# The four convolution products of the second token group: from VectorE to GpSimd

## Chip, cores and metric

The kernel runs on one core of a Trainium2 chip. The metric is the device time of one execution in microseconds (us), lower is better; three runs of the kernel before are given with their median.

## The reference

What is computed is a convolution with weights of its own for each token, followed by a two-layer MLP. Cut to what matters:

```python
# x [4, 4096, 192], weight_gen [4, 4096, 8, 7]
w = softmax(weight_gen, axis=-1)              # 7 taps for each token and head
x_unf = x_pad[:, idx, :]                      # the token and the 6 before it
out = einsum('bshk,bskhg->bshg', w, x_unf)    # g = 24 channels a head
h = out.reshape(16384, 192) @ w_in            # w_in [192, 2048]
g = s * max(h, 0) ** 2 + b
return g @ w_out                              # w_out [2048, 192]
```

Everything is float32. The kernel holds each factor of a matmul as a rounded part and a rest, and adds three products.

## The kernel before

The 16384 tokens are cut into 32 groups of 512. For each group the convolution is formed on 128 partitions (4 quarters of the channels times 32 runs of 16 tokens), turned, split into its two parts, and then multiplied with `w_in` (the tiles `ph`), passed through relu and square on ScalarE (`r`, `gh`) and VectorE (`gl`), and multiplied with `w_out` (the tiles `po`). The 2048 hidden channels are taken in four quads of 512, each of two pairs of 128.

The order on every engine is the order of the program text, written out by hand. There are three stretches that matter here:

- The first group (index 0) has a convolution of its own kind, with TensorE (`first_pieces`).
- While the first group goes through the MLP, in the loop `for i in range(NC)` with its eight turns, the weights are converted as they arrive: `convert(i)` splits the tile of weights `r` into `wc`'s two parts, with five instructions on VectorE (lines 239, 243, 247, 254 and 258; from the sixth tile on a sixth, line 266), three on ScalarE (236, 252, 277) and a few matmuls (276). Turn `i` of the loop also holds the pair's matmuls (`mm1_pair`, lines 542 and 548, and `mm2_pair`, line 634), relu and square (578, 582, 586) and `low_g` (604). A pair's second matmul group trails the first by one turn.
- Between these, the convolution of the second group (index 1) is laid by the tuple `beside`, which says which of the group's pieces follow each turn.

From the second group's MLP on, the loop `for n in range(NQ, last + 1)` runs 124 quads of the same kind (`mm1_quad`, line 567, and `mm2_quad`, line 652), each with some pieces of the convolution of a later group.

The convolution's pieces are in `conv_pieces(g)`. `products(h, k0, k1)` multiplies the shifted input `xt` by the tap weights `w` into the tile `pr`, for one of the two heads of each quarter and the taps k0 to k1: 4 taps by 16 tokens by 24 channels, 1536 elements a partition, or 3 taps, 1152. There are four such instructions a group (line 351). `add` sums the taps. For the second group alone, where `by_dma` is true, the adds are DMAs from GpSimd's queue that accumulate into `pr` (line 363), and the pieces stand in this order:

```python
softmax_a, exp, softmax_b,
products(0, 0, 4), products(1, 0, 4), add(0, 2, 2), products(0, 4, 7), products(1, 4, 7),
add(4, 5), add(0, 1), add(4, 6), last_add,
transposes, split_hi, split_lo,
```

with

```python
beside = ((0, 3), (3, 4), (4, 6), (6, 11), (11, 11), (11, 13), (14, 15), (15, 15))
```

so the softmax follows turn 0, the first product turn 1, the second product and the first DMA turn 2, the last two products and the other three DMAs turn 3, and the last add (line 376) with the transposes (387, 392) turn 5.

Of the kernel before, what the change touches and what calls it, by code (L numbers as in the profile page):

```python
# [20 lines left out]
def dynamic_conv_then_relu2_mlp(  # L21
# [24 lines left out]
    nc = tc.nc  # L46
# [264 lines left out]
    def conv_pieces(g):  # L311
        st = {}
        by_dma = g == 1
# [29 lines left out]
        def products(h, k0, k1):  # L343
            def f():
                if "pr" not in st:
                    st["pr"] = conv.tile([P, K, J, FQ], F32, tag="pr", name="pr")
                xt, w, pr = xt_t[g], st["w"], st["pr"]
                xs = xt[:, k0:k0 + 1, h * G:h * G + 1]
                ws = w[:, 0:1, h:h + 1, k0:k0 + 1]
                n = k1 - k0  # L350
                nc.vector.tensor_tensor(  # L351
                    out=pr[:, k0:k1, :, h * G:(h + 1) * G],
                    in0=bass.AP(xs.tensor, xs.offset, [xs.ap[0], [FQ, n], [FQ, J], [1, G]]),
                    in1=bass.AP(ws.tensor, ws.offset, [ws.ap[0], [1, n], [HQ * K, J], [0, G]]),
                    op=ALU.mult,
                )
            return f
# [464 lines left out]
```

## Time and profile before

| | us |
|---|---|
| median of three runs | 1161.42 |
| lowest, highest run | 1161.0, 1163.08 |
| span of the profiled execution, first to last instruction | 1161.6 |

The profiled execution's own time is not listed apart from the three runs; its span is 0.2 us over their median.

How to read it: the profile lists instructions by engine. PE is TensorE's matmuls and PEld its weight loads, DVE is VectorE, ACT is ScalarE, POOL is GpSimd, SP is SyncE, which issues most DMAs. L351 is line 351 of the kernel. Times are counted from the span's start. "Idle before" a row is how long its engine had stood still, and the arrow names what it waited for. POOL's spans are rough.

### The profile page before, as it was taken

What the parts mean: (1) busy time and instruction counts of PE and PEld (TensorE: products, weight loads), DVE (VectorE), ACT (ScalarE), POOL (GpSimd) and SP (SyncE); (2) the same over time, 40 slices, a digit from 0 to 9 for tenths busy, and PEclk for the clock granted to TensorE, in tenths of its full rate; (3) what the DMA queues carried; (4) which work ended last, traced back from release to release, by engine and by line L of the source; (5) the groups of instructions that cost most, each with busy time, mean ns of one, the idle gap of its engine ahead of it and who ended that gap; (6) DMA issues with size and microseconds to landing.
All of it is one profiled execution on the core that took longest, in us unless ns stands there. A gap on an engine that the chain in (4) does not pass through costs nothing.

```text
span 1161.6 us, 29979 instructions
## 1 busy us (share of the span) xinstructions
PE 1142.1 (98%) x12724; PEld 1125.3 (97%) x12724; DVE 943.1 (81%) x1346; ACT 848.9 (73%) x898; POOL 9.7 (1%) x28
## 2 busy tenths in 40 slices
PE   7999999999999999999999999999999999999997
PEld 5679999999999999999999999999999999999997
DVE  6988888878898878898878898887888887888854
ACT  3867777777777777777777777777777777777774
POOL 0000000000000000000000000000000000000000
PEclk9999999999999999999999999999999999999999
DMA  5651122212122212112212112222212221212110
GB/s 150 160 92 40 29 41 47 46 33 47 25 37 46 47 34 47 26 37 47 47 33 46 29 36 45 47 43 37 38 31 41 47 47 33 47 25 38 24 25 15
DMA packets 171738, 52.33 MB, mean 45 GB/s; under 512 B 160148, under 2 KB 163860, under 8 KB 171604
## 3 DMA queue, kind: packets, MB, share of 16 engines
q1 hardware_dynamic: 171028, 48.45, 21.2%
q0 software_dynamic: 576, 1.97, 0.9%
q8 instruction: 100, 1.64, 0.6%
q14 instruction: 34, 0.28, 0.1%
HBM read 27.70 MB, written 12.58 MB: 35 GB/s over the span
## 4 chain that ended last, share of the span: by engine, by line
PE 94%; DVE 3%; DMA 1%; ACT 1%; issue 0%; SPq 0%; DVEq 0%
PE po L652 48%; PE ph L567 43%; PE po L634 1%; PE po L457 1%; DVE gl L604 1%; DVE pr L351 1%; DMA r<-in_moe_w_in_dram 0%; DVE r L247 0%; DMA x<-in_x_dram 0%; DVE v L258 0%; DVE t L254 0%; PE ph L542 0%; PE ph L276 0%; PE po L476 0%; DVE t L243 0%
## 5 line engine op out<-in xcount | busy, mean ns | idle before, releaser
L652 PE MATMUL po<-wc,gh 64*128 64x384 f32 x3936 | 596.2, 354 | 0.3 <-DVE y L669 0.3
L652 PEld LDWEIGHTS po<-wc,gh 64*128 64x128 f32 x3936 | 570.9, 184 | 0.8 <-DVE y L669 0.6
L652 PE MATMUL po<-wc,gl 64*128 64x192 f32 x3936 | 550.0, 249 | 0.0
L652 PEld LDWEIGHTS po<-wc,gl 64*128 64x128 f32 x3936 | 549.1, 187 | 0.1
L604 DVE SCALAR_TENSOR_TENSOR gl<-r,shift,gh 128x1024 fp32r<-128x1024 f32 x256 | 327.0, 1278 | 185.3 <-ACT gh L586 183.5
L578 ACT ACTIVATE r<-ph 128x1024 f32<-128x1024 f32 x254 | 247.2, 1023 | 264.5 <-PE ph L567 260.9
L567 PE MATMUL ph<-xa,wc 64*128 64x512 f32 x2976 | 374.9, 387 | 0.0
L567 PEld LDWEIGHTS ph<-xa,wc 64*128 64x128 f32 x2976 | 343.0, 184 | 1.2 <-ACT r L582 0.3
L586 ACT ACTIVATE gh<-r,shift 128x1024 fp32r<-128x1024 f32 x254 | 292.8, 1153 | 8.1
L582 ACT ACTIVATE r<-r 128x1024 f32<-128x1024 f32 x254 | 267.2, 1052 | 0.2
L567 PE MATMUL ph<-xb,wc 64*128 64x512 f32 x1488 | 205.0, 386 | 0.1
L351 DVE TENSOR_TENSOR pr<-xt,w 128x1536 f32<-128x1536 f32 (+1 forms) x124 | 187.5, 1552 | 1.6 <-DVE w L336 0.4
L567 PEld LDWEIGHTS ph<-xb,wc 64*128 64x128 f32 x1488 | 179.1, 184 | 0.8 <-issue 0.5
L368 DVE TENSOR_TENSOR pr<-pr 128x1536 f32<-128x1536 f32 (+1 forms) x120 | 136.1, 1154 | 2.1
L664 DVE TENSOR_SCALAR u<-po,ratio 128x192 f32<-128x192 f32 x128 | 49.7, 409 | 2.0 <-PE po L634 1.9
L669 DVE SCALAR_TENSOR_TENSOR y<-po,ratio,u 128x192 f32<-128x192 f32 x128 | 49.6, 408 | 0.1
L376 DVE TENSOR_TENSOR acc<-pr 128x768 f32<-128x768 f32 x31 | 29.7, 958 | 1.0
L387 DVE STREAM_TRANSPOSE xT<-acc 128x128 f32<-128x128 f32 x124 | 27.6, 280 | 1.1
L392 DVE STREAM_TRANSPOSE xT<-acc 128x128 f32<-128x128 f32 x124 | 26.3, 270 | 0.0
L634 PE MATMUL po<-wc,gh 128*128 128x384 f32 x80 | 24.4, 369 | 0.0
L405 DVE TENSOR_TENSOR xb<-xT,xb 128x512 fp32r<-128x512 f32 x31 | 21.2, 685 | 0.0
L405 DVE TENSOR_TENSOR xa<-xT,xa 128x512 fp32r<-128x512 f32 x31 | 21.2, 685 | 0.0
(67 smaller groups left out, 346.0 us busy)
## 6 DMA issues: line engine op xcount, KB each, us to landing
xt<-in_x_dram SPq DMA_DIRECT2D x120, 132.0 KB, 3.1
out_dram<-y SPq DMA_DIRECT2D x124, 96.0 KB, 1.9
xb<-xb SPq DMA_DIRECT2D x124, 64.0 KB, 2.0
wg<-in_weight_gen_dram SPq DMA_DIRECT2D x124, 28.0 KB, 2.6
r<-in_moe_w_out_dram SPq DMA_DIRECT2D x8, 384.0 KB, 4.2
r<-in_moe_w_in_dram SPq DMA_DIRECT2D x12, 128.0 KB, 6.0
pr<-pr POOLq DMA_DIRECT2D x3, 384.0 KB, 4.3
r<-in_moe_w_in_dram SPq DMA_DIRECT2D x32, 32.0 KB, 2.8
```

Source lines behind the costliest of these rows:

```text
L351: nc.vector.tensor_tensor(out=pr[:, k0:k1, :, h * G:(h + 1) * G], in0=bass.AP(xs.tensor, xs.offset, [xs.ap[0], [FQ, n], [FQ, J], [1, G]]), ...
L368: nc.vector.tensor_tensor(out=pr[:, o:o + n], in0=pr[:, o:o + n], in1=pr[:, a:a + n], op=ALU.add)
L405: nc.vector.tensor_tensor(out=x[h][:, 1], in0=xT[:, h], in1=x[h][:, 0].bitcast(F32), op=ALU.subtract)
L567: nc.tensor.matmul(out=h_t[n, p][:, j], lhsT=w1(2 * k + p, part, block, j, rows), rhs=v[rows], start=(at < 2 and c == 0), stop=(at >= 4 an ...
L578: nc.scalar.activation(out=r[p], in_=h_t.pop((n, p)), func=AF.Relu)
L582: nc.scalar.activation(out=r[p], in_=r[p], func=AF.Square)
L586: nc.scalar.activation(out=gh, in_=r[p], func=AF.Identity, bias=shift)
L604: nc.vector.scalar_tensor_tensor(out=gl, in0=sq, scalar=shift, in1=gh.bitcast(F32), op0=ALU.add, op1=ALU.subtract)
L634: nc.tensor.matmul(**m)
L652: nc.tensor.matmul(**m)
L664: nc.vector.tensor_scalar(out=u[i], in0=o_t[g][tiles[i]][:, 1, :], scalar1=ratio, scalar2=None, op0=ALU.mult)
L669: nc.vector.scalar_tensor_tensor(out=y[:, t], in0=o_t[g][t][:, 0, :], scalar=ratio, in1=u[i - 1], op0=ALU.mult, op1=ALU.add,)
```

## The change

In `products`, the multiplication is issued on GpSimd for the second group, and on VectorE for the groups from the third on, as before. Operands, pieces and `beside` stay as they are.

```diff
@@ -348,7 +348,7 @@
                 xs = xt[:, k0:k0 + 1, h * G:h * G + 1]
                 ws = w[:, 0:1, h:h + 1, k0:k0 + 1]
                 n = k1 - k0
-                nc.vector.tensor_tensor(
+                (nc.gpsimd if by_dma else nc.vector).tensor_tensor(
                     out=pr[:, k0:k1, :, h * G:(h + 1) * G],
                     in0=bass.AP(xs.tensor, xs.offset, [xs.ap[0], [FQ, n], [FQ, J], [1, G]]),
                     in1=bass.AP(ws.tensor, ws.offset, [ws.ap[0], [1, n], [HQ * K, J], [0, G]]),
```

On VectorE, after turns 1 and 2 of the loop over the weight tiles, one product stood each time between `low_g` (L604) and the next tile's conversion (L239 and on); shown is the place after turn 2, the one after turn 1 reads alike.

```order
 L258 SCALAR_TENSOR_TENSOR v<-r,t 128x768
 L604 SCALAR_TENSOR_TENSOR gl<-r,shift,gh 128x1024
-L351 TENSOR_TENSOR pr<-xt,w 128x64x24
 L239 TENSOR_SCALAR t<-t 128x768
 L243 TENSOR_SCALAR t<-t 128x768
```

The product is gone there, and the conversion follows `low_g` directly. After turn 3 VectorE had the last two products in the same place:

```order
 L266 TENSOR_TENSOR rest<-r,wc_110 128x768
 L604 SCALAR_TENSOR_TENSOR gl<-r,shift,gh 128x1024
-L351 TENSOR_TENSOR pr<-xt,w 128x48x24 x2
 L239 TENSOR_SCALAR t<-t 128x768
 L243 TENSOR_SCALAR t<-t 128x768
```

On GpSimd, whose own order has nothing else between the identity matrix of the start (`eye_f`) and the DMAs that add, the four products come in ahead of the DMAs that read them.

```order
 L282 ISA
 L282 AFFINE_SELECT eye_f<-ones_f 128x128
+L351 TENSOR_TENSOR pr<-xt,w 128x64x24 x2
 L363 DMA pr<-pr 128x1536
+L351 TENSOR_TENSOR pr<-xt,w 128x48x24 x2
 L363 DMA pr<-pr 128x768 x3
 L162 MEMSET xt 1x288 x16
```

GpSimd is not held back by the turns of the loop as VectorE's order was: its first product is due as soon as the tap weights `w`, the input `xt` and the tile `pr` are ready.

## Rows read from the trace of the kernel before

**Rows 1.** Page, part 1: busy us, share of the span and instructions, by engine.

```profile
PE 1142.1 (98%) x12724; PEld 1125.3 (97%) x12724; DVE 943.1 (81%) x1346; ACT 848.9 (73%) x898; POOL 9.7 (1%) x28
```

**Rows 2.** Windows: stretch, length, busy by engine (instructions), TensorE clock, DMA share, GB/s.

```profile
40.00:50.00 10.00, 10.00 (x52) 7.29 (x51) 9.69 (x11) 8.20 (x11) 0.00 (x0) 1.00 0.53 155
50.00:60.00 10.00, 9.09 (x54) 7.58 (x54) 9.76 (x12) 8.33 (x9) 1.40 (x2) 1.00 0.74 127
60.00:70.00 10.00, 7.48 (x37) 6.16 (x35) 9.62 (x13) 6.29 (x7) 2.22 (x3) 0.83 0.78 151
```

**Rows 3.** Chain that ended last, 42 to 92 us: start, length, engine, line.

```profile
42.72 1.67 DVE pr L351
...
49.30 1.67 DVE pr L351
...
56.75 2.54 DVE pr L351 x2
...
64.02 1.62 PE ph L276 x4
...
91.90 4.07 PE po L652 x26
```

**Rows 4.** Timeline of PE, 41 to 79 us: start, length, count, [idle before, releaser].

```profile
41.09 0.94 PE L276 MATMUL ph<-r,eye_f 128*128 128x384 f32 x2
...
55.70 0.41 PE L276 MATMUL ph<-rest,eye 128*128 128x384 f32 x1 [0.91 <-DVE rest L266]
...
64.02 0.66 PE L276 MATMUL ph<-rest,eye 128*128 128x384 f32 x1 [2.52 <-DVE rest L266]
...
68.43 1.56 PE L542 MATMUL ph<-xa,wc 128*128 128x512 f32 x6
...
70.81 0.44 PE L276 MATMUL ph<-rest,eye 128*128 128x384 f32 x1
...
73.86 1.55 PE L542 MATMUL ph<-xa,wc 128*128 128x512 f32 x6
...
78.67 3.04 PE L567 MATMUL ph<-xa,wc 64*128 64x512 f32 x24
```

**Rows 5.** Windows of 1 us, columns as in rows 2: the clock around the longest stall.

```profile
62.00:63.00 1.00, 0.00 (x0) 0.00 (x0) 0.95 (x2) 0.28 (x1) 0.00 (x0) 1.00 1.16 224
63.00:64.00 1.00, 0.00 (x0) 0.01 (x1) 1.00 (x3) 0.96 (x2) 0.00 (x0) 0.79 1.03 197
64.00:65.00 1.00, 0.98 (x3) 1.00 (x4) 1.00 (x2) 0.97 (x2) 0.84 (x1) 0.50 1.05 203
66.00:67.00 1.00, 1.00 (x6) 1.00 (x5) 0.96 (x2) 1.00 (x2) 0.00 (x0) 0.50 1.04 203
67.00:68.00 1.00, 1.00 (x9) 1.00 (x8) 0.86 (x3) 1.00 (x2) 0.00 (x0) 1.00 0.50 92
```

**Rows 6.** Timeline of DVE, columns as in rows 4: from the tap weights on.

```profile
37.38 0.40 DVE L336 TENSOR_TENSOR w<-e,sm 128x224 f32<-128x224 f32 x1
37.69 0.55 DVE L239 TENSOR_SCALAR t<-t 128x768 f32<-128x768 f32 x1
...
40.57 0.96 DVE L258 SCALAR_TENSOR_TENSOR v<-r,t 128x768 fp32r<-128x768 uint32 x1
41.45 1.28 DVE L604 SCALAR_TENSOR_TENSOR gl<-r,shift,gh 128x1024 fp32r<-128x1024 f32 x1
...
70.77 0.95 DVE L376 TENSOR_TENSOR acc<-pr 128x768 f32<-128x768 f32 x1
```

**Rows 7.** Timeline of POOL, columns as in rows 4: all that it computes before 241 us.

```profile
0.85 0.10 POOL L178 MEMSET space<- 128x1 f32 x1
0.88 0.21 POOL L281 MEMSET ones_f<- 128x128 f32 x1
1.16 0.29 POOL L282 TENSOR_SCALAR_AFFINE_SELECT eye_f<-ones_f 128x128 f32<-128x128 f32 x1
...
51.60 1.00 POOL L363 DMA_DIRECT2D pr<-pr  x1 [50.15 <-DVE t L239]
59.60 1.76 POOL L363 DMA_DIRECT2D pr<-pr  x2 [7.00 <-DVE pr L351]
64.16 0.86 POOL L363 DMA_DIRECT2D pr<-pr  x1 [2.79 <-DMA pr<-pr]
```

**Rows 8.** Line 363, the adding DMAs: time from issue to landing.

```profile
DMA to landing us min/median/max: 3.8/4.8/6.7
```

## The prediction

> **What bounds the kernel now.** I read the page's busy times first, then the same by windows, then the chain that ended last, then single rows. The page shows PE busy for 98% of the span and POOL for 1% [rows 1], so from there a change of VectorE's load would seem to be worth nothing. The windows show that this is an average: between 40 and 70 us VectorE is busy 9.69, 9.76 and 9.62 us of each 10, while PE falls from 10.00 to 7.48 [rows 2]. In the chain all four products of the second group lie on the path: 1.67, 1.67 and 2.54 us, 5.88 in all, the last of them before the matmul that PE begins at 64.02 [rows 3]. From 91.90 us on the chain is the quads' matmuls, to the end. So whatever the change does is decided between 37 and 79 us, and what PE gains or loses at the first quad (78.67 us, rows 4) is handed to the end: the waits between 79 and 92 us hang on PE's own results, and nothing that the change touches lies there.
>
> **What the change removes.** VectorE loses 5.88 us of chain. PE can take less than that, because it takes only its own losses. These are its two stalls on VectorE, 0.91 us at 55.70 and 2.52 us at 64.02 [rows 4], and the slow clock that follows the second: granted 0.79 in the last microsecond of the stall and 0.50, the 1.2 GHz level, for the three that follow, 1.00 again from 67 [rows 5]. What that clock costs is read from the same work at both levels: from the conversion matmul to the next pair's first is 64.02 to 68.43, 4.41 us, and a turn later 70.81 to 73.86, 3.05 us [rows 4]. The difference is 1.36. The sum is 0.91 + 2.52 + 1.36 = **4.79 us**, the most that I give the change. Late next would be PE itself. The loss of cover elsewhere costs nothing: with the products gone, the adding DMAs start earlier, not later, and the last add that reads them stands at 70.77 [rows 6].
>
> **What it adds.** Four products on GpSimd, two of 1536 elements a partition and two of 1152. No row shows a product there, so I bound it by the nearest rows [rows 7]. Below: memset writes 1 element in 0.10 us and 128 in 0.21, 0.87 ns an element, which makes 1.43 and 1.10 us, 5.1 us for four. The only GpSimd row that also reads a tensor is the select, 0.29 us for 128 elements; in proportion 3.48 and 2.61 us, **12.2 us** for four. Above: the product reads two tensors, and on VectorE 768 elements take 0.96 us with two (L258) against 0.55 with one (L239) [rows 6], 1.75 times as long; that ratio on 12.2 makes 21.3 us. I take 12.2, the row that does most of the same work. The Trainium skill, "GPSIMD Engine Reference", section 3.1, speaks against moving elementwise work there: it gives 4497 ns for an addition of 2048 elements, from which I estimate 3.4 and 2.5 us, 11.8 us for four; by it the forecast below would be 0.4 us lower. No run here shows that figure yet.
>
> **Whether GpSimd's time is its own.** For dependencies it is. The tap weights are ready at 37.78 us (37.38 + 0.40, rows 6) and GpSimd has nothing else to do. The first two products would end at 37.78 + 6.96 = 44.7, the first DMA is issued in 1.00 us, and the other two products end near 51.0. Then the adds that wait for each other: a DMA issue of about 0.9, 4.8 to landing, 0.9 and 4.8 again [rows 7, 8], at 62.4, against the last add at 70.77, or about 66 if PE gains all it can. So the product's length alone is covered.
>
> The open point is VectorE beside it. In exactly this time VectorE streams from the same memory without a pause, and its rows look as if it used both of two read paths nearly always: the one-tensor operation on 768 elements takes 0.55 us where the two-tensor one takes 0.96 [rows 6], so a single tensor is read at about the rate of two. If GpSimd reads by one of these paths and holds it for a whole instruction, then VectorE's next instruction waits for the end of it, and takes a turn between two products. VectorE then stands still for GpSimd's 12.2 us, in place of the 5.88 that it computed itself. The earlier start makes it worse: all four products fall into the conversion of one weight tile, from 37.7 to 42.7, where before they were spread over three turns of the loop.
>
> The price of that, step by step. PE's conversion matmul at 41.09 comes 12.2 later, at 53.29. From there to the first quad PE needs what it needed before, 78.67 - 41.09 = 37.58 us, without its two stalls and their slow clock, since VectorE now is ahead of it: 37.58 - 4.79 = 32.79. A stall of 12 us lowers the clock at least as much as one of 2.52 did, so 1.36 comes back. The first quad begins at 53.29 + 32.79 + 1.36 = 87.44, against 78.67: **8.8 us later**. In general the change costs the blocked time less 3.4 us, and gains 4.79 where nothing is blocked. With the bounds: 5.1 us blocked makes +1.7, 21.3 makes +17.9.
>
> What POOL's rows say of this is little: its first adding DMA took 1.00 us to issue beside VectorE's work, and no VectorE row there is longer for it; but that instruction need not read the tensors. Below zero is not excluded by any row, so both ends stay. I take the blocked case, because GpSimd has to read 2 x (1536 + 1152) elements a partition from a memory that VectorE's rows show being read at the double rate all the time.
>
> The Trainium skill, "SBUF — State Buffer", section "Who interferes with whom", states this mechanism: VectorE and GpSimd share one pair of ports; a VectorE instruction with two SBUF inputs or in a two-port mode and a GpSimd instruction that reads SBUF exclude each other for a whole instruction. By that rule the sum is +8.8; without it it is -4.79. No run here shows it yet.
>
> **The rivals.**
>
> *Nothing is blocked.* GpSimd works beside VectorE at no cost. For it: POOL's DMA issues lengthened no VectorE row. Against it: the double rate. PE loses its stalls and the slow clock, 4.79 us, and the time is 1161.4 - 4.8 = 1156.6. This is the other side. It decides where blocked time stays under 3.4 us: below that the stalls removed outweigh it.
>
> *VectorE is slowed in part.* Only some kinds of its instructions exclude GpSimd, or the two share. With 2 to 6 us of VectorE time lost, the formula gives -1.4 to +2.6: 1160.0 to 1164.0.
>
> *GpSimd is the one held off.* VectorE's instructions follow each other within some 0.03 us, and GpSimd may only come in where VectorE stops. Taking the 5.88 us freed, spread over the three turns, it would end its 12.2 us of work after 70, the two DMA rounds after it need 11.4, and the last add waits until about 82. Behind that add stand the transposes, the split and a `low_g` in VectorE's order; between the add and the first quad lie about 4.4 us of VectorE and ScalarE work, so the quad begins near 86, 7.7 us late: 1169. The place is then the last add, not the conversion.
>
> *Heavier products.* With the upper bound the blocked case gives 1161.4 + 17.9 = 1179.3.
>
> That the change doesn't do what it says I rule out: the order shows the four products on GpSimd, ahead of their DMAs, and gone from VectorE.
>
> **How the numbers follow.** The sum is made against a span of 1161.6, which is 0.2 us over the median of the runs; I count from the median, 1161.4. A measurement of this kernel can tell about 0.2%, 2.3 us, from no change. Blocked for about 8.5 to 15.5 us of VectorE time, 1166.5 to 1173.5: chance 0.38, and its middle, 1161.4 + 8.8 = **1170.2**, is the forecast. Nothing blocked, 1156.6: 0.28. Slowed in part: 0.16, of which 0.03 is faster by over 0.2%, 0.10 within and 0.03 slower. GpSimd held off: 0.07. Heavier: 0.11. So faster is 0.28 + 0.03 = 0.31, the same 0.10, slower 0.38 + 0.07 + 0.11 + 0.03 = 0.59. The range from 1156.4 to 1173.8 leaves out the heavier products and the ends of the other cases, about 0.15. Cases of both signs are in it; the likeliest one's own range is 1166.5 to 1173.5.
>
> **What would show it.** In the profile of the changed kernel: four POOL rows of line 351 from about 38 us, 3.5 and 2.6 us long; beside them VectorE rows of lines 243, 247 or 254 several times as long, or preceded by idle time of 2 to 3.5 us; PE idle before line 276 near 41 us by some 12 us, the clock at 0.50 after it; no stall at lines 276 with `rest` afterwards; the first quad near 87 us. The prediction is wrong if VectorE's rows keep 0.55 and 0.96 us beside GpSimd's: then the first quad stands near 74. If POOL's rows are stretched instead, or the last add waits for a DMA, it was GpSimd that was held off.

## Result and profile after

| | before | after |
|---|---|---|
| median of five runs, us | 1161.56 | 1170.06 |
| lowest, highest, us | 1161.0, 1163.54 | 1168.97, 1170.9 |
| span of the profiled execution, us | 1161.6 | 1168.5 |

The change makes the kernel slower: the ratio is 1.0061, with a 95% interval of 1.0050 to 1.0072, so 5.8 to 8.4 us. The profiled execution of the changed kernel took 1170.16 us, 1.7 over its span; if that holds for the kernel before as well, its profiled execution took about 1163.3 us, near the longest of its five runs, while the prediction counts from 1161.4. The two spans differ by 6.9 us.

The page of the changed kernel, part 1, to be held against [rows 1]:

```profile
PE 1143.3 (98%) x12724; PEld 1125.8 (96%) x12724; DVE 947.6 (81%) x1342; ACT 848.8 (73%) x898; POOL 20.4 (2%) x32
```

VectorE lost four instructions (1346 to 1342), and yet is busy 4.5 us longer. Where that lies, the timelines of POOL and DVE show:

```profile
37.69 6.13 POOL L351 TENSOR_TENSOR pr<-xt,w 128x1536 f32<-128x1536 f32 x2 [36.24 <-DMA r<-in_moe_w_in_dram]
44.14 1.01 POOL L363 DMA_DIRECT2D pr<-pr  x1 [0.32 <-POOL pr L351]
44.91 4.61 POOL L351 TENSOR_TENSOR pr<-xt,w 128x1152 f32<-128x1152 f32 x2
...
53.98 1.03 POOL L363 DMA_DIRECT2D pr<-pr  x1 [2.39 <-DMA pr<-pr]
```

```profile
37.97 3.13 DVE L243 TENSOR_SCALAR t<-t 128x768 uint32<-128x768 uint32 x1
41.14 3.50 DVE L247 SCALAR_TENSOR_TENSOR r<-r,t 128x768 uint32<-128x768 uint32 x1
44.67 5.28 DVE L254 TENSOR_SCALAR t<-r 128x768 uint32<-128x768 uint32 x1
50.05 0.96 DVE L258 SCALAR_TENSOR_TENSOR v<-r,t 128x768 fp32r<-128x768 uint32 x1
...
78.89 0.95 DVE L376 TENSOR_TENSOR acc<-pr 128x768 f32<-128x768 f32 x1
```

Three neighbouring VectorE instructions take 3.13, 3.50 and 5.28 us. A few us later the same lines have 0.56, 0.96 and 0.64 us again. In the kernel before, at the same weight tile, they were:

```profile
38.28 0.56 DVE L243 TENSOR_SCALAR t<-t 128x768 uint32<-128x768 uint32 x1
38.91 0.96 DVE L247 SCALAR_TENSOR_TENSOR r<-r,t 128x768 uint32<-128x768 uint32 x1
39.90 0.56 DVE L254 TENSOR_SCALAR t<-r 128x768 uint32<-128x768 uint32 x1
```

Against these they are 2.57, 2.54 and 4.72 us too long, 9.83 in all. Each ends shortly after a product does: the first product runs to 40.68 and L243 ends at 41.10; the fourth runs to 49.52 and L254 ends at 49.95. The row of L258 that starts after the last product has its old length.

What PE makes of it, against [rows 4]:

```profile
44.74 0.91 PE L276 MATMUL ph<-r,eye_f 128*128 128x384 f32 x2 [3.88 <-issue]
...
51.07 0.69 PE L276 MATMUL ph<-v,eye 128*128 128x384 f32 x1 [5.02 <-DVE v L258]
...
57.01 1.55 PE L542 MATMUL ph<-xa,wc 128*128 128x512 f32 x6
...
72.13 0.41 PE L276 MATMUL ph<-rest,eye 128*128 128x384 f32 x1 [0.37 <-DVE rest L266]
...
86.11 3.03 PE L567 MATMUL ph<-xa,wc 64*128 64x512 f32 x24
```

PE stands still for 3.88 and 5.02 us at the fourth weight tile, where it had no stall before. The stalls at the sixth and seventh tiles, 0.91 and 2.52 us in [rows 4], have shrunk to nothing and 0.37. The first quad begins at 86.11, in place of 78.67: 7.44 us later. The clock, in windows with the columns of rows 2:

```profile
46.00:47.00 1.00, 0.05 (x1) 0.00 (x0) 1.00 (x1) 0.00 (x0) 1.00 (x1) 0.50 0.96 197
...
55.00:56.00 1.00, 1.00 (x6) 1.00 (x5) 0.96 (x2) 1.00 (x2) 0.02 (x1) 0.50 0.80 144
56.00:57.00 1.00, 1.00 (x8) 1.00 (x7) 1.00 (x2) 1.00 (x2) 0.00 (x0) 0.90 1.20 372
```

It is granted 0.50, the 1.2 GHz level, for ten microseconds, against three in [rows 5]; PE works in about five of them. From the quads on both kernels run alike: a quad's `po` matmuls take 4.55 and its `ph` matmuls 4.09 us of the chain in either.

### The profile page after: what moved, and what is told of

Same layout as the page of the kernel before. It is cut to its first block, busy times and chain, and to the rows that moved or that the text cites. A ratio compares the mean times of both kernels' runs of the same rounds, so it can differ in the third digit from the quotient of the medians.

```text
span 1168.5 us, 29980 instructions
## 1 busy us (share of the span) xinstructions
PE 1143.3 (98%) x12724; PEld 1125.8 (96%) x12724; DVE 947.6 (81%) x1342; ACT 848.8 (73%) x898; POOL 20.4 (2%) x32
## 4 chain that ended last, share of the span: by engine, by line
PE 94%; DVE 2%; DMA 1%; SPq 1%; ACT 1%; issue 0%; DVEq 0%; ACTq 0%
PE po L652 48%; PE ph L567 43%; PE po L634 2%; PE ph L276 1%; SPq L217 1%; DMA r<-in_moe_w_out_dram 1%; DMA r<-in_moe_w_in_dram 1%; DVE t L254 1%; PE ph L542 0%; DVE r L247 0%; DVE gl L604 0%; DVE t L243 0%; PE ph L548 0%; ACT gh L586 0%; DMA wg<-in_weight_gen_dram 0%
## 5 line engine op out<-in xcount | busy, mean ns | idle before, releaser
L652 PEld LDWEIGHTS po<-wc,gh 64*128 64x128 f32 x3936 | 561.0, 184 | 0.8 <-DVE y L669 0.6
L604 DVE SCALAR_TENSOR_TENSOR gl<-r,shift,gh 128x1024 fp32r<-128x1024 f32 x256 | 327.1, 1278 | 184.3 <-ACT gh L586 182.1
L567 PE MATMUL ph<-xb,wc 64*128 64x512 f32 x1488 | 201.3, 386 | 0.0
L351 DVE TENSOR_TENSOR pr<-xt,w 128x1536 f32<-128x1536 f32 (+1 forms) x120 | 181.4, 1554 | 1.2
L567 PEld LDWEIGHTS ph<-xb,wc 64*128 64x128 f32 x1488 | 175.8, 184 | 0.4
L368 DVE TENSOR_TENSOR pr<-pr 128x1536 f32<-128x1536 f32 (+1 forms) x120 | 136.1, 1155 | 2.1
L162 POOL MEMSET xt<- 1x288 f32 x16 | 5.3, 331 | 1019.2 <-PE po L652 1018.6
```

The source lines that it names most:

```text
L351: (nc.gpsimd if by_dma else nc.vector).tensor_tensor(out=pr[:, k0:k1, :, h * G:(h + 1) * G], in0=bass.AP(xs.tensor, xs.offset, [xs.ap[0], ...
L368: nc.vector.tensor_tensor(out=pr[:, o:o + n], in0=pr[:, o:o + n], in1=pr[:, a:a + n], op=ALU.add)
L567: nc.tensor.matmul(out=h_t[n, p][:, j], lhsT=w1(2 * k + p, part, block, j, rows), rhs=v[rows], start=(at < 2 and c == 0), stop=(at >= 4 an ...
L604: nc.vector.scalar_tensor_tensor(out=gl, in0=sq, scalar=shift, in1=gh.bitcast(F32), op0=ALU.add, op1=ALU.subtract)
L652: nc.tensor.matmul(**m)
```

## The experiments

The **theory** is that of the prediction: while GpSimd reads for its product, VectorE's instructions that use the second path of reads wait for the end of it. The **rivals**: any GpSimd work slows VectorE; only the two-tensor product does; the blocking is real, but it is the place (four products inside one conversion) and not its sum that costs.

All experiments start from the kernel before. The traces' start-up differs from that of the kernel before by up to 1.1 us, so the table counts from the same place in each, PE's matmul of line 542 that waits for the third weight tile, to the first quad (one profiled execution each; the ratio is of all runs). In the kernel before it is this row:

```profile
39.06 1.20 PE L542 MATMUL ph<-xa,wc 128*128 128x512 f32 x4 [0.65 <-ACT wc L277]
```

and so 78.67 - 39.06 = 39.61 us.

| kernel | L542 | first quad | between | over before | ratio to before, 95% interval |
|---|---|---|---|---|---|
| before | 39.06 | 78.67 | 39.61 | | |
| the change | 38.76 | 86.11 | 47.35 | +7.74 | 1.0061 (1.0050 to 1.0072) |
| removal alone | 37.92 | 73.37 | 35.45 | -4.16 | 0.9965 (0.9952 to 0.9979) |
| first product alone | 39.12 | 78.86 | 39.74 | +0.13 | 1.0008 (0.9999 to 1.0017) |
| three-tap products alone | 39.00 | 81.74 | 42.74 | +3.13 | 1.0029 (1.0017 to 1.0041) |
| products one by one | 38.54 | 80.97 | 42.43 | +2.82 | 1.0040 (1.0026 to 1.0054) |
| products twice | 39.79 | 88.84 | 49.05 | +9.44 | 1.0086 (1.0071 to 1.0101) |

**The removal alone.** Each product keeps one token of 16, on VectorE.

```diff
-                    out=pr[:, k0:k1, :, h * G:(h + 1) * G],
+                    out=pr[:, k0:k1, 0:1 if by_dma else J, h * G:(h + 1) * G],
```

(and `J` likewise in the two inputs; `pr` is the first group's tile, taken over)

> Leaves out 15 of the 16 tokens of each of the second group's four products (VectorE forms the sixteenth at the old place), so nothing is added on GpSimd and the adding DMAs keep their place. This is the removal alone. Theory: VectorE's work shrinks by about 4.9 us (four rows of 0.2 to 0.3 us stay of 5.88), PE's stalls at 55.7 and 64.0 us and the slow clock behind the second go, and the first quad begins at 74 to 75.5 us, the time is 3 to 5 us under before. Rival (the weights' DMAs are late next, as ScalarE waited 2.9 us for them in the run with the fills): PE keeps a wait at one of the last three tiles and the first quad begins at 76.5 to 78 us, 0.5 to 2 us under before.

```profile
37.92 1.20 PE L542 MATMUL ph<-xa,wc 128*128 128x512 f32 x4 [0.56 <-ACT wc L277]
...
73.37 3.04 PE L567 MATMUL ph<-xa,wc 64*128 64x512 f32 x24
```

Measured: 4.16 us less up to the first quad, and 1158.07 against 1162.57 us. Of PE's stalls on VectorE 0.37 us is left and the clock stays at 1.00. The theory's size holds; no wait for weights takes the stalls' place.

**Zeros instead of products.**

```diff
+                if by_dma:
+                    nc.gpsimd.memset(pr[:, k0:k1, :, h * G:(h + 1) * G], 0.0)
+                    return
```

> Leaves out the four products of the second group: GpSimd fills their places in pr with zeros instead, so it only writes. Theory (GpSimd's reading shuts out VectorE's instructions that use a second path): VectorE's two-tensor rows L247, L258, L604 keep 0.96, 0.96 and 1.28 us beside the fills; at most the one-tensor rows at double rate (L239, L243, L254) wait for a fill. Nearly all of the removal's gain shows: first quad at 74 to 75 us against 78.67 before and 86.11 with the change, time 4 to 5 us under before, if the fills shut out nothing; 2 us less gain for each 2 us that L243 or L254 wait. Rival (any GpSimd work slows VectorE, by the memory's rate): all kinds of rows grow beside the fills, and the first quad is not before 78.

The fills need neither weights nor input, so they ran at once when `pr` was free, from 22.42 us, and the adding DMAs with them, from 25.43. Beside them on VectorE:

```profile
22.58 0.69 DVE L489 TENSOR_TENSOR xa<-po,xa 128x512 fp32r<-128x512 f32 x1 [2.78 <-ACT xa L484]
23.19 0.68 DVE L489 TENSOR_TENSOR xb<-po,xb 128x512 fp32r<-128x512 f32 x1
23.88 1.65 DVE L239 TENSOR_SCALAR t<-t 128x768 f32<-128x768 f32 x1
25.57 3.36 DVE L243 TENSOR_SCALAR t<-t 128x768 uint32<-128x768 uint32 x1
```

```profile
22.42 2.70 POOL L352 MEMSET pr<- 128x1536 f32 x2 [20.98 <-PE po L476]
...
26.12 2.38 POOL L352 MEMSET pr<- 128x1152 f32 x2
```

So writing alone shuts out the one-tensor rows at double rate, 1.65 and 3.36 us in place of 0.56. The rows that read one of their tensors from PSUM (L489) kept 0.69 and 0.68. No row with two tensors in SBUF fell beside a fill, so that part of the expectation was not put to the test. The first quad stands at 78.55 us, far from the 74 to 75 of fills that shut out nothing, and the time is that of before (1.0005, 0.9995 to 1.0014). The two rows are 3.9 us too long, about what the removal gives, as the expectation's clause on L243 and L254 has it. ScalarE also waits 2.90 us for a weight tile, while the adding DMAs run early; what that wait adds was not tried. The rival's first quad did come, not before 78, but its "all kinds of rows" is refuted by L489.

**Copies instead of products.**

```diff
+                if by_dma:
+                    nc.gpsimd.tensor_copy(
+                        out=pr[:, k0:k1, :, h * G:(h + 1) * G],
+                        in_=bass.AP(xs.tensor, xs.offset, [xs.ap[0], [FQ, n], [FQ, J], [1, G]]),
+                    )
+                    return
```

> Leaves out the multiplication by the tap weights in the second group: GpSimd copies the shifted input into the four places of pr, so it reads one tensor and writes one. Theory (reading shuts VectorE out for the whole instruction): VectorE rows beside a copy end when the copy ends, as beside the products; the delay equals the copies' own length, about half of the products', so 5 to 6 us in place of 9.8, and the first quad at 81 to 83 us. Rival (two-input products are what excludes): no row of VectorE grows, first quad at 74 to 75 us, 4 to 5 us under before.

These too started before the tap weights, as soon as the input was there: two from 34.40 to 38.06 us and two from 39.07 to 41.62. VectorE's softmax stood beside them:

```profile
35.07 0.38 DVE L319 TENSOR_REDUCE mx<-wg 128x32 f32<-128x224 f32 x1
35.48 1.24 DVE L321 TENSOR_TENSOR e<-wg,mx 128x224 f32<-128x224 f32 x1
37.18 0.39 DVE L332 TENSOR_REDUCE sm<-e 128x32 f32<-128x224 f32 x1 [0.46 <-ACT e L327]
37.60 0.49 DVE L333 TENSOR_SCALAR sm<-sm 128x32 f32<-128x32 f32 x1
38.13 0.35 DVE L334 RECIPROCAL sm<-sm 128x32 f32<-128x32 f32 x1
38.52 3.35 DVE L336 TENSOR_TENSOR w<-e,sm 128x224 f32<-128x224 f32 x1
```

The two-tensor rows L321 and L336 take 1.24 and 3.35 us in place of 0.39; the reduces keep 0.38 and 0.39 beside the same copies. One tensor read is enough, which refutes the rival. The first quad did not come late (78.67, not 81 to 83): the rows add only 4.1 us (0.85, 0.31 and 2.96), about what the removal gives, so the time is the same (1.0009, 0.9999 to 1.0018).

**The products twice.** GpSimd forms them, and VectorE again at the old places.

```diff
+                if by_dma:
+                    nc.gpsimd.tensor_tensor(
...
+                        op=ALU.mult,
+                    )
                 nc.vector.tensor_tensor(
```

> The products of the second group are formed twice, by GpSimd and again by VectorE in its old places. Theory: the change is a removal (worth 4.8 us) plus a blocking (9.8 us of VectorE), which add up; with the removal undone VectorE's chain is 9.8 us later at the last weight tile, and the first quad stands at 88 to 90 us, the time 9 to 11.5 us over before. Rival (the loss is the start of all four inside one conversion, with its stall and slow clock, and VectorE's own work is hidden under PE by then): the first quad stays near 86, within 1 us of the change.

The first quad stands at 88.84 and the time is 10 us over before, both within the theory's ranges. That removal and blocking simply add up is not shown: counted from L542, the change's 7.74 and the removal's 4.16 would make 11.9 us, and the run has 9.44, 1.7 more than the change. GpSimd's last two products came later here, behind the first adding DMA, beside an L243 that then took 5.68 us, so the blocking has another place too; with the two rows at the fourth tile, 3.13 and 3.50 us again, it is 10.2 us.

**The products one by one.** Each reads its weights from a copy made on VectorE at the old place (the copies take 0.19 us for four taps, 0.27 for the two of three).

```diff
+                if by_dma:
+                    wk = conv.tile([P, J, n], F32, tag=f"wk{h}{k0}", name="wk")
+                    nc.vector.tensor_copy(out=wk, in_=w[:, :, h, k0:k1])
+                    ws = wk[:, 0:1, 0:1]
+                    nc.gpsimd.tensor_tensor(
...
+                    return
```

> As the change, but each GpSimd product reads its tap weights from a small copy that VectorE makes at the product's old place, so the products start one by one, after turns 1, 2 and 3. Theory: blocked time counts wherever VectorE is saturated: 2.6, 2.6 and 4.7 us of blocking and four copies of about 0.2 us, against 5.88 us removed, so VectorE is 4.8 us late at the last weight tiles and the first quad begins at 83 to 85 us, 4.5 to 6 us over before. Rival (place): the loss came from four products inside one conversion; spread, PE's work covers them, and the first quad begins before 80.

Its first quad began at 82.42, but its time was 1182.04 us, 1.0171 of before (1.0154 to 1.0188): from there on every quad took 4.19 + 4.58 us, not 4.09 + 4.55:

```profile
515.90 4.58 PE po L652 x34
520.48 4.19 PE ph L567 x36
```

The copies' tiles, 896 bytes a partition, had moved all tiles behind them. So it was run again with the filler tile `space` smaller by as much:

```diff
-    LEAD, GAP = 440, 512
+    LEAD, GAP = 440, 288
```

> As the spread run, with the filler tile made smaller by the 896 bytes of the four copies, so that the tiles behind keep their addresses. First quad as there, at 82 to 83 us. Theory of the rest of that run (its tiles moved, and every quad's matmuls took 8.77 us in place of 8.64): each quad takes 8.64 us again and the time is 3 to 4.5 us over before. Rival (the later quads are slowed by something the products do): 15 us or more over before again.

The quads are back at 4.09 + 4.55 us, and the time is 1.0040 of before: the products do nothing to the later quads. Its blocked rows are L243 and L247:

```profile
42.81 3.14 DVE L243 TENSOR_SCALAR t<-t 128x768 uint32<-128x768 uint32 x1
...
50.41 3.16 DVE L243 TENSOR_SCALAR t<-t 128x768 uint32<-128x768 uint32 x1
...
58.98 2.43 DVE L243 TENSOR_SCALAR t<-t 128x768 uint32<-128x768 uint32 x1
61.44 2.83 DVE L247 SCALAR_TENSOR_TENSOR r<-r,t 128x768 uint32<-128x768 uint32 x1
```

They are 8.9 us too long together, nearly the 9.83 of the change, but up to the first quad this trace is 2.82 us over before, not 7.74 (the trace with the moved tiles 82.42 - 39.04 = 43.38, 3.77 over). Neither theory nor rival named that: by the traces, part of the change's loss is the place. How much is less sure than 7.74 - 2.82 = 4.9 us, because the profiled execution, 1164.90 us, is the shortest of four with a median of 1167.78. By the ratios the loss is about 4.7 us (3.0 to 6.3) against the change's 7.1 (5.8 to 8.4), so some 2.4 us for the place, and the two intervals meet. PE's stalls are 2.58 and 2.37 us there, at the sixth and seventh tile, where it stood before as well.

**Half and a quarter.** The condition alone differs:

```diff
-                nc.vector.tensor_tensor(
+                (nc.gpsimd if by_dma and k0 == 4 else nc.vector).tensor_tensor(
```

for the three-tap products, and `(h, k0) == (0, 0)` for the first product alone.

> Half of the change: the two products of three taps go to GpSimd, those of four stay on VectorE. GpSimd's order puts them behind the first adding DMA, which waits for VectorE's second product, so they run from about 52 us beside the sixth tile's conversion. Theory: 4.7 us of blocking against 2.54 us removed, in a later place with PE at work behind it: VectorE 2.2 us later at the stall of 64 us, first quad at 80 to 81.5 us, time 1.5 to 3.5 us over before. Rival (all of the loss is the early place): first quad at or under 78.7 us.

> A quarter of the change: the first product of four taps alone goes to GpSimd and runs from 37.7 us beside the fourth tile's conversion. Theory: 2.6 us of blocking against 1.67 us removed: VectorE 0.9 us later from there on, first quad at 79.3 to 80.5 us, time 0.5 to 2 us over before. Rival (below 3.4 us of blocking the removed stalls outweigh it, as my sum says): first quad at 77.5 to 78.3 us, time 0.5 to 1 us under before.

The half costs 3.13 us, and its first quad, 81.74, is just above the expected range; L247 took 5.77 us beside its two products. The quarter moved the first quad by 0.13 us and its time can't be told from before: VectorE was 0.9 us later at the seventh tile (64.95 against 64.02 in [rows 4]), but this time the stall there, 2.39 us, left the clock at 1.00, which gave that back. The rival's first quad, under 78.3, did not come. It does not settle the sum of the prediction, though: that sets the blocking against all 5.88 us taken from VectorE, and here only 1.67 were.

**The later groups on GpSimd.** `nc.gpsimd if g > 1`, the second group on VectorE.

> The second group's products stay on VectorE, those of the third group and all later ones go to GpSimd, where PE is the bound and VectorE has 17% of its time free. Theory: the exclusion works there as well: beside GpSimd's 10.7 us a group, rows with two tensors in SBUF (L604, L368, L405, L321, L336) and one-tensor rows at double rate grow up to 3 us, reduces (L319, L332), transposes and rows that read PSUM (L664, L669) don't; VectorE's load goes from 83% to 85 to 96%, PE gets stalls of 0 to 1.5 us a group, time between the same and 45 us over before. Rival (only a saturated VectorE makes it dear, and the place alone was wrong): VectorE's rows keep their lengths, its load falls to about 66%, time within 0.2% of before.

The time was 1291.86 us, 11% over before, far outside. One group's products and the VectorE rows beside them:

```profile
514.50 6.76 POOL L351 TENSOR_TENSOR pr<-xt,w 128x1536 f32<-128x1536 f32 x2 [25.46 <-PE po L652]
524.48 4.43 POOL L351 TENSOR_TENSOR pr<-xt,w 128x1152 f32<-128x1152 f32 x2 [3.22 <-PE po L652]
```

```profile
510.90 0.39 DVE L336 TENSOR_TENSOR w<-e,sm 128x224 f32<-128x224 f32 x1
515.20 3.30 DVE L604 SCALAR_TENSOR_TENSOR gl<-r,shift,gh 128x1024 fp32r<-128x1024 f32 x1 [3.90 <-ACT gh L586]
...
519.07 0.40 DVE L669 SCALAR_TENSOR_TENSOR y<-po,ratio,u 128x192 f32<-128x192 f32 x1
519.40 0.40 DVE L664 TENSOR_SCALAR u<-po,ratio 128x192 f32<-128x192 f32 x1
...
528.94 1.76 DVE L368 TENSOR_TENSOR pr<-pr 128x1536 f32<-128x1536 f32 x1 [6.60 <-POOL pr L351]
```

The exclusion is there as expected: L604 with two tensors in SBUF takes 3.30 us, the rows that read PSUM keep 0.40. Beside it stands a wait that I had not counted: the adds (L368) wait 6.6 us in each group for products that GpSimd begins late, because GpSimd itself waits for PE. The tap weights are ready at about 511.3 us, but the first products begin at 514.50 and the last two after another wait of 3.22 us; most of the 25.46 us before is time in which nothing was due. In GpSimd's order `hand_over` has put instructions that wait for PE's sums, and the products stand behind them. How the 130 us divide between blocking and wait was not tried: PE stands still for 78 us in all until `gl` (L604) is there, and in VectorE's order `gl` is both a blocked row and a row behind the waiting adds.

**Relief of VectorE in another way.** As VectorE is the bound up to 64 us, work was moved from it to PE: `LATE` (line 73) says from which tile on VectorE forms a rest (L266) in place of a third product on PE.

```diff
-    LATE = 5
+    LATE = 7
```

> Products as before the change; the rest of the weight tile (L266, 0.87 us on VectorE) is formed by VectorE for the eighth tile alone and by PE's third product for the sixth and seventh, so VectorE is relieved by 1.75 us ahead of PE's stall at 64 us and PE gets two times 1.2 us more work. Theory (VectorE's chain to 64 us is the bound before): stall at 55.7 gone, the one at 64.0 about 1 us or less, first quad 0.5 to 2 us earlier, time 0 to 2 us under before. Rival (PE's own work is the bound there): 1 us or more over before.

> Products on VectorE as before the change; PE's third product takes the rest of the sixth weight tile alone, so VectorE is 0.87 us earlier at the next tile and PE has 1.2 us more work. Theory: PE's stall at 55.7 is gone, the one at 64.0 shrinks to about 1.5 us and leaves the clock at 1.00; first quad at 76.2 to 77 us (77.16 with two tiles moved), time 1 to 2.5 us under before. Rival (a stall of 1.5 us also lowers the clock): first quad at 77.5 to 78.5 us, time within 1 us of before.

With 7 the first quad begins at 77.16 us, 1.81 us earlier than before when counted from L542; the stall at 64 is gone and the ratio is 0.9987 (0.9978 to 0.9995): a small gain, and the only kernel of the study with the whole computation that beats before. With 6 it is 76.71 us, 1.62 earlier from L542, the stall 1.57 us with the clock at 1.00, and the ratio, 0.9992 (0.9983 to 1.0001), can't be told from 1.

## Why the prediction was right

The time is 1170.06 us for 1170.2 forecast, and the mechanism is the one forecast. That the two agree to 0.14 us is luck: the forecast was 8.8 us over before, and the ratio makes it 7.1 (5.8 to 8.4), the first quad 7.44. Its terms are less good than their sum:

- **The removal**, 4.79 us: measured by itself 4.16. PE was the next bound, as said.
- **GpSimd's length**, 12.2 us from the select's row [rows 7]: 6.13 and 4.61, 10.7 us. The estimate from the Trainium skill, "GPSIMD Engine Reference", section 3.1, was 11.8; this case's products were faster still, 2.99 us for the first with 1536 elements.
- **The blocking**, 12.2 us by the forecast: VectorE's rows are 9.83 us too long. It gets in before the first product takes hold (L239, 0.55 us), beside the DMA's issue, and once between products. The rule of the Trainium skill, "SBUF — State Buffer", section "Who interferes with whom", is borne out in what it excludes: two tensors in SBUF or a double rate against a GpSimd instruction that reads (L243, L247, L254 here, L321 and L336 in the copies' run), and not the reduces or the rows reading PSUM.
- **The slow clock**, 1.36 us: too small. The same work, from the fourth tile's first matmul with `v` to the next pair's first, takes 57.01 - 51.07 = 5.94 us after and 45.49 - 42.04 = 3.45 before, 2.49 more. The rows before, beside the 51.07 and 57.01 shown above:

```profile
42.04 0.34 PE L276 MATMUL ph<-v,eye 128*128 128x384 f32 x1
...
45.49 1.55 PE L542 MATMUL ph<-xa,wc 128*128 128x512 f32 x6
```

- **The place.** That the early start makes it worse fits the traces: spread, nearly the same blocking costs 2.82 us in place of 7.74; by the times the gap is smaller. The rule "the blocked time less 3.4" would give 6.4 for the 9.83 us measured, where the first quad shows 7.44; for small blocked times no run tests it.

The sum as measured, along PE: its matmul with `v` comes at 51.07 in place of 42.04, 9.03 us late; the clock takes 2.49 more; and 86.11 - 51.07 = 35.04 against 78.67 - 42.04 = 36.63 up to the first quad says that 1.59 + 2.49 = 4.08 were won back. 9.03 + 2.49 - 4.08 = 7.44. The forecast's 8.8 was 12.2 + 1.36 - 4.79: too much blocking and too little clock, which partly cancelled.

Of the rivals, "nothing is blocked" is refuted by the rows and "GpSimd held off" as well: the last adding DMA is issued at 53.98, and the last add, at 78.89, follows VectorE's `low_g` without a wait. "Heavier products" is refuted by their length, 10.7 us and not 21.3. "Slowed in part" expected 2 to 6 us lost and has its size wrong, but it was right that only some kinds of instructions are held: reduces and rows reading PSUM are not.

## What to carry to other kernels

Moving work from a saturated VectorE to GpSimd is no relief if VectorE's instructions beside it read two tensors from SBUF, or one at the double rate: VectorE then waits out GpSimd's instructions, here 9.8 us for 5.9 us of its own work. Look first at which of VectorE's instructions would stand beside (reduces and rows reading PSUM went on undisturbed), and where a wait would find the other engines with nothing else to do. Instructions in GpSimd's order wait behind each other, so one that synchronises with PE holds up all products behind it.

## What was not expected of the hardware

- VectorE was let in between two products of four taps, in the change and with the products formed twice, but not between two of three taps: L254 waited through both (5.28 us), and so did L243 with the products formed twice (5.68) and L247 with the half (5.77). Only in the run with products one by one, where the second of the two has a wait of its own for its weights' copy, was VectorE let in between (L243 2.43, L247 2.83 us). The taps need not be the reason. Each row that waited through both began while the adding DMA was being issued, before the first of the two products: L254 at 44.67, the product at 44.91. So did the rows that waited through both three-tap fills (L243, 25.57 before 26.12) and both three-tap copies (L336, 38.52 before 39.07). Each row that waited for one alone began when that product, fill or copy was already running. Which of the two decides was not tried.
- GpSimd's writing alone stretched VectorE's double-rate rows, 0.56 to 3.36 us.
- A shift of tiles by 896 bytes a partition made every quad's matmuls 1.5% longer (8.77 for 8.64 us), some 16 us over 124 quads; with the addresses put back it was gone.
- A stall of 2.52 us lowered the clock in the kernel before, and one of 2.39 with the first product alone did not.
